# Batch 1's queries and keys re-cut: a shorter first part transposed together with the end of batch 0, and a last block of 96 tokens in step 23

## The chip, the core and the metric

One core of a Trainium2 chip (trn2) runs the whole program. The metric is device time in microseconds (us) of one execution; the median of three runs is the figure given. PE is the matmul engine (TensorE), DVE the vector engine, ACT the scalar engine, POOL the GpSimd engine, SP the engine that only issues transfers. PSUM is the memory that PE writes and that ACT and DVE copy out of.

## The reference

Attention over a window of 32 tokens to either side for 8 batches, 8 heads, 576 tokens and head size 64, then a two-layer block with an ELU on the 4608 x 512 result:

```
scores = q @ k.T / sqrt(64), outside |i - j| <= 32 set to -1e9
attn   = exp(scores - max) / (sum + 1e-9)
x      = (attn @ v), heads side by side: 4608 x 512
h      = x @ w_in                      # 512 x 2048
g      = where(h > 0, h, exp(min(h, 0)) - 1)
out    = g @ w_out                     # 2048 x 512
```

## The kernel before

The tokens are cut into 36 pairs of 2 x 64 queries; a batch of 576 tokens is 4.5 pairs, so pair 4 holds the last 64 queries of batch 0 and the first 64 of batch 1, and pair 5 holds queries 64 to 191 of batch 1. One pair is `scores` (L371, 16 small matmuls), `exponential` (L392, ACT), `mask` (L399, DVE), `pv` (L408, 16 small matmuls), `normalize` (L422, DVE), and then a transpose of the result on PE with a copy out of PSUM (`x_transpose` L433 and `x_evac` L450) or, from pair 10 on, by a transfer.

The two-layer block runs in 144 steps (loop at L840). Step kk does `elu` of the step before on DVE, then `mm1(kk)` (eight matmuls of 256 columns, L734), `exponents` (ACT, L744), `subtract` (L756), and then `mm2` of an earlier step (four matmuls of 512 columns, L787). The work of the pairs, the casts, the transposes and the later loads are put by hand between these: `at(kk, slot, fn, ...)` (L568) files a task, and the loop runs it. The slots of one step stand in this order: "first", `elu`, "dve", the first half of mm1, "half", the second half of mm1 and its `exponents` and `subtract`, "mid", then the mm2's (a slot that is a number stands ahead of the mm2 of that number: in step 8 slot 6 lies between mm2(5) and mm2(6)), "end". Each engine keeps this order; nothing is reordered later.

q and k come in token-major and are needed head-size-major. Tokens are placed so that partition c of 32 holds nj tokens that follow each other, and one 128-column transpose is made for each j of nj. There are two ways in. `load_cast` (L137) lets POOL issue a transfer that casts to bf16; each j then takes two transposes of 64 columns (L335). `load_qk` (L123) lets SP load fp32, `cast_qk` (L294) casts on ACT or DVE, and each j takes one full transpose (L340). `transpose_qk` (L327) makes the transposes into one PSUM tile and copies that tile into `qT` or `kT` with one copy (`evict`, L344, on the engine that it is given; with `later` the copies come after all the transposes).

Batch 1 is cut into two halves of 288 tokens: `HALF_A = (0, 9)` by `load_cast` (L548), transposed in step 8 (q, slot 6) and step 9 (k, slot "half"), both copied out by ACT; `HALF_B` by `load_qk` (L559), cast in steps 14 and 15, transposed at the end of steps 15 and 16. The last 64 queries and 32 keys of batch 0 (`FRONT_C`) are transposed by `transpose_late` (L592) in step 6. Pair 4's `scores` and `exponential` stand at the end of step 9, pair 5's in step 12, pairs 6 and 7 from step 18, pairs 8 and 9 from step 26 (L621 to L641).

PSUM tiles go by tag, and each tag has one buffer: "s" and "u" hold 1024 fp32 for each of 128 partitions and serve the pairs' scores and results and the transposes; "h0" and "h1" serve mm1 of even and odd steps. A tile of a tag is written only when the copy or the read of that tag's last tile is done. From pair 6 on, even pairs use "s" and odd pairs "u", and `x_transpose` writes into its pair's tag: pair 7's is filed at the end of step 22, in "u". In steps 22 to 25 batch 2's q and k are transposed in four groups of nine, with the tags "s", "u", "s", "u" (steps 22 mid, 23 end, 24 mid, 25 mid), all copied out by ACT.

POOL issues its transfers in the order of the code: batch 1's two casting loads lie between parts of w_in and w_out and ahead of batch 1's v. SP waits at a small transfer (`gate`, L191) for the last part of w_in, and then issues HALF_B of batch 1 and the whole of batch 2.

Of the kernel before, what the change touches and what calls it, by code (L numbers as in the profile page):

```python
# [10 lines left out]
BF16 = mybir.dt.bfloat16  # L11
# [4 lines left out]
def _bap(ap, new_ap, off=0):  # L16
    return bass.AP(tensor=ap.tensor, offset=ap.offset + off,
                   ap=[list(x) for x in new_ap])
# [3 lines left out]
def kernel(  # L22
# [9 lines left out]
    nc = tc.nc  # L32

    B, H, S, D = q.shape
# [9 lines left out]
    HP = H // 2  # L44
    NC = 128 // HP
# [15 lines left out]
    cpool = ctx.enter_context(tc.tile_pool(name="const", bufs=1))  # L61
# [32 lines left out]
    def ps_tile(shape, dt, tag, name):  # L94
        return pools[tag].tile(shape, dt, tag=tag, name=name)
# [21 lines left out]
    HJ = SJ // 2  # L117
    WHOLE, HALF_A, HALF_B = (0, SJ), (0, HJ), (NC * HJ, HJ)
    FRONT_B = ((NC * HJ, HJ - 2), (NC * HJ, HJ - 1))
    FRONT_C = ((NC * (SJ - 2), 2), (NC * (SJ - 1), 1))  # L120
    qk_f = {}

    def load_qk(b, which, part, engs=(nc.sync, nc.sync)):  # L123
        z, nj = part
        mj = max(nj, HJ)
        t = lpool.tile([128, 2, mj * D], FP32, tag=f"f{which}{mj}",
                       name=f"f{which}", bufs=2 if part is WHOLE else 1)
        qk_f[b, which, z] = t
        src = (q, k)[which][b, :, z:z + NC * nj, :].rearrange(
            "(g h) (c j) d -> c g h (j d)", h=2, j=nj)  # L130
        for h in range(2):
            engs[h].dma_start(out=t[:, h, 0:nj * D], in_=src[:, :, h, :])
# [4 lines left out]
    def load_cast(b, which, part):  # L137
        z, nj = part
        mj = nj if nj < 3 else HJ + 1
        t = cpool.tile([128, 2, mj * D], BF16, tag=f"c{which}{mj}",  # L140
                       name=f"c{which}")[:, :, 0:nj * D]
        qk_c[b, which, z] = t
        src = (q, k)[which][b, :, z:z + NC * nj, :].rearrange(
            "(g h) (c j) d -> c g h (j d)", h=2, j=nj)
        nc.gpsimd.dma_start(out=t, in_=src)

    def load_v(b, m, rows=(0, 128)):
        lo = 128 * m - WIN
        p0 = max(rows[0], -lo)
        p1 = min(rows[1], S - lo)  # L150
        nc.gpsimd.dma_start(  # L151
            out=V_e[b % 3][p0:p1, m, :, 0:D],
            in_=v[b, :, lo + p0:lo + p1, :].rearrange("h p d -> p h d"))
# [37 lines left out]
    def gate(src, dt=BF16, eng=nc.sync):  # L191
        gates[0] += 1
        t = cpool.tile([1, 1], dt, name=f"gate{gates[0]}")
        eng.dma_start(out=t, in_=src)

    def load_w_in(c, z=0, nz=1):
        w = D_FF // 4 // nz
        c = c * nz + z
        nc.gpsimd.dma_start(
            out=w_in_sb[:, :, c * w:(c + 1) * w],  # L200
            in_=moe_w_in[:, c * w:(c + 1) * w].rearrange(
                "(o p) f -> p o f", p=128))

    def load_w_out(c, z=0, nz=1):
        n = NFO // 4 // nz
        c = c * nz + z
        nc.gpsimd.dma_start(
            out=w_out_sb[:, c * n:(c + 1) * n, :],
            in_=moe_w_out[c * n * 128:(c + 1) * n * 128, :].rearrange(
                "(o p) f -> p o f", p=128))  # L210

    def w_in_at(c):
        return w_in_sb[0:1, 0, (c + 1) * (D_FF // 4) - 1:(c + 1) * (D_FF // 4)]
# [7 lines left out]
    def edges(i):  # L221
# [8 lines left out]
    ident = cpool.tile([128, 128], BF16)  # L230
# [15 lines left out]
        out=far, in_=far, compare_op=ALU.is_ge, fill=FAR,  # L246
        base=0, pattern=[[0, 2], [-1, QB]], channel_multiplier=1)
    nc.gpsimd.affine_select(
        out=far, in_=far, compare_op=ALU.is_ge, fill=FAR,
        base=2 * WIN, pattern=[[0, 2], [1, QB]], channel_multiplier=-1)  # L250
    nc.gpsimd.affine_select(
        out=far[:, 0, :], in_=far[:, 0, :], compare_op=ALU.is_ge, fill=FAR,
# [35 lines left out]
    def copy_on(eng, d_, s_):  # L288
        if eng is nc.scalar:
            nc.scalar.copy(d_, s_)  # L290
        else:
            eng.tensor_copy(d_, s_)  # L292
# [15 lines left out]
    def keys_or_queries(b, which):  # L308
        if which == 0:
            return qT[b % 2].rearrange("p g s -> p (g s)")  # L310
        return kT[b % 2][:, KPAD:KPAD + HP * S]
# [15 lines left out]
    def transpose_qk(b, which, part, j0, n, evac, tag="t0", later=None,  # L327
                     pt=None):
        z, nj = part
        if pt is None:  # L330
            pt = ps_tile([128, 1024 if n <= 8 else 2048], BF16, tag, "ptx")
        for j in range(n):
            if (b, which, z) in qk_c:
                for h in range(2):
                    nc.tensor.transpose(  # L335
                        pt[64 * h:64 * (h + 1), j * 128:(j + 1) * 128],
                        qk_c[b, which, z][:, h, (j0 + j) * D:
                                          (j0 + j + 1) * D], ident)
            else:
                nc.tensor.transpose(  # L340
                    pt[:, j * 128:(j + 1) * 128],
                    qk_b[b, which, z][:, j0 + j, :], ident)

        def evict(d=None, rows=NC, pitch=S):  # L344
            d = keys_or_queries(b, which) if d is None else d
            copy_on(evac,
                    _bap(d, [d.ap[0], [pitch, HP], [nj, rows], [1, n]],
                         z + j0),
                    _bap(pt, [pt.ap[0], [1, HP], [HP, rows], [128, n]]))

        if later is None:
            evict()
        else:
            later.append(evict)
# [132 lines left out]
    for which in range(2):  # L487
        load_cast(0, which, FRONT_B[which])
# [9 lines left out]
    for which in range(2):  # L498
        load_cast(0, which, FRONT_C[which])
    load_w_out(1)  # L500
# [3 lines left out]
    BOTH = (nc.scalar, nc.vector)  # L504
# [40 lines left out]

    load_w_in(2, 0, 2)
    for which in range(2):
        load_cast(1, which, HALF_A)  # L548
    load_w_in(2, 1, 2)
    load_w_out(2)  # L550
    for m in range(3):
# [2 lines left out]
    load_w_out(3)  # L554
    for m in range(3, VS):
        load_v(1, m)
    gate(w_in_at(3))
    for which in range(2):
        load_qk(1, which, HALF_B)  # L559
    for which in range(2):  # L560
        load_qk(2, which, WHOLE)

# [5 lines left out]
    def at(kk, slot, fn, *args):  # L568
        tasks.setdefault((kk, slot), []).append((fn, args))
# [19 lines left out]
    at(1, "mid", x_transpose, 3, "y1")  # L589
    at(1, "mid", x_evac, 3, nc.vector)  # L590
    at(5, "dve", swap_pools)
    def transpose_late(tag):  # L592
        pt = ps_tile([128, 2, 512], BF16, tag, "ptx")
        evicts = []
        for which in range(2):
            transpose_qk(0, which, FRONT_C[which], 0, FRONT_C[which][1],
                         BOTH[which], later=evicts, pt=pt[:, which, :])
        for evict in evicts:
            evict()

    at(6, "mid", transpose_late, "s")
    at(6, "dve", rotate_back, 0, 3, 4, (1,))

    for which in range(2):
        at(8 + which, (6, "half")[which], transpose_qk, 1, which, HALF_A, 0,
           HJ, nc.scalar, "s")
        at(14 + which, "mid", cast_qk, 1, which, HALF_B, 0, HJ, BOTH[which])
        at(15 + which, "end", transpose_qk, 1, which, HALF_B, 0, HJ,
           nc.scalar, "s")
    at(6, "dve", edges, 2)  # L610
    at(16, "dve", hold_v, 2)
# [12 lines left out]
    for i in range(4, NPAIR):  # L624
        two = i >= FIRST_TWO
        kk, z = begin[i], i % 2 if two else 0
        at(kk, "end" if i == 4 else "mid", scores, i,
           "u" if z else "s")
        at(kk + z, "end" if i == 4 else "mid", exponential, i)
        at(kk + 1 + z, "dve", mask, i)  # L630
        at(kk + (2 if two else 1), "end", pv, i)
        n = kk + (3 + z if two else 2)
        at(n, "dve", normalize, i)
        if i < FIRST_DMA:

            x_at = (n + 1, "half") if i == 5 else (n, "end")
            at(*x_at, x_transpose, i)
            at(*x_at, x_evac, i, nc.scalar)
        else:
            at(n, "end", x_dma, i)  # L640
# [248 lines left out]
```

## Time and profile before

| what | value |
|---|---|
| median of three runs | 302.49 us (302.11 to 302.96) |
| the profiled execution's own time | 302.52 us |
| its span, first to last instruction | 300.8 us |
| PE busy | 291.8 us, 97% of the span |
| DVE busy | 240.9 us, 80% |
| ACT busy | 170.2 us, 57% |
| granted clock of PE | 0.999 |
| casting loads of batch 1 (q and k) | 288 KB each, 8.2 and 8.3 us from issue to landing |
| loads of HALF_B (q, k) | issued at 39.70 and 41.03 us, 4.8 to 5.1 us to landing |

A line of the timeline holds the start (us from the span's start), the duration, the engine, the line of the code, the operation, what is written from what, the shapes and the count. "[0.42 <-PE ps L734]" says that the engine stood idle for 0.42 us before it and what ended that. A matmul's duration runs to its end in the pipeline, so it is longer than its slot: the distance from one start to the next says what PE spends. Some matmul records are missing, so a group of four can read "x3" and start late.

### The profile page before, as it was taken

How to read it: one execution, taken by the hardware profiler on the slowest of the kernel's cores; microseconds unless marked ns; L12 is line 12 of the kernel's file. 1: busy time of each engine (PE TensorE's matmuls, PEld its weight loads, DVE VectorE, ACT ScalarE, POOL GpSimd, SP SyncE). 2: the span in 40 equal slices, each digit the busy share in tenths (PEclk: the TensorE clock that was granted, in tenths of full speed). 3: DMA queues.
4: the chain of work that ended last, by engine and by line, in shares of the span. 5: the costliest groups of instructions: out<-in, count | busy, mean ns of one | idle time of the engine just before them, and what ended most of it. 6: DMA issues, size and time to landing. Idle time of an engine off the chain costs nothing.

```text
span 300.8 us, 7664 instructions
## 1 busy us (share of the span) xinstructions
PE 291.8 (97%) x3066; PEld 198.6 (66%) x3118; DVE 240.9 (80%) x479; ACT 170.2 (57%) x258; POOL 52.7 (18%) x74
## 2 busy tenths in 40 slices
PE   7899999999999999999999999999999999999995
PEld 3585567677666666666666666666666666666673
DVE  7788588978787988888889789887988787877773
ACT  3783648688655567456745665467535353534342
POOL 8777203520005000410032002300000000000000
PEclk9999999999999999999999999999999999999999
DMA  9999999999957978999899989997921111111011
GB/s 190 168 200 203 185 233 349 370 179 231 241 159 199 239 116 270 244 267 135 161 256 323 172 203 252 312 153 137 268 54 72 35 72 38 70 37 70 2 70 71
DMA packets 94070, 52.68 MB, mean 175 GB/s; under 512 B 78163, under 2 KB 83795, under 8 KB 94035
## 3 DMA queue, kind: packets, MB, share of 16 engines
q1 hardware_dynamic: 47330, 35.61, 44.7%
q0 software_dynamic: 44976, 10.10, 44.2%
q10 hardware_dynamic: 1728, 6.49, 6.3%
q8 instruction: 24, 0.39, 0.6%
q14 instruction: 12, 0.09, 0.1%
HBM read 36.70 MB, written 15.34 MB: 173 GB/s over the span
## 4 chain that ended last, share of the span: by engine, by line
PE 85%; DMA 5%; issue 3%; DVE 2%; ACT 2%; POOL 2%; POOLq 0%; ACTq 0%; DVEq 0%
PE ps L734 39%; PE psY L787 38%; PE psS L416 4%; DMA out_dram<-y_sb 3%; PE psS L384 3%; DMA c<-in_k_dram 2%; ACT e_sb L744 1%; DVE g_sb L767 1%; PE ptx L335 1%; PE psXT L438 1%; POOL Vo L158 1%; DVE qkb L292 0%; ACT qkb L290 0%; PE ptx L340 0%; PE psS L364 0%
## 5 line engine op out<-in xcount | busy, mean ns | idle before, releaser
L744 ACT ACTIVATE e_sb<-ps 128x512 f32<-128x512 f32 (+1 forms) x145 | 86.3, 596 | 113.4 <-PE ps L734 106.0
L734 PE MATMUL ps<-xT,w_in_sb 128*128 128x256 bf16 (+1 forms) x1168 | 149.7, 271 | 0.1
L787 PE MATMUL psY<-w_out_sb,g_sb 128*128 128x512 bf16 (+2 forms) x541 | 139.3, 373 | 2.9 <-issue 0.3
L734 PEld LDWEIGHTS <-w_in_sb 128*128 128x128 bf16 x1168 | 110.4, 98 | 36.8 <-issue 0.8
L767 DVE SCALAR_TENSOR_TENSOR g_sb<-ps,m_sb 128x512 bf16<-128x512 f32 (+1 forms) x145 | 99.3, 686 | 13.1 <-DVE m_sb L756 0.5
L756 DVE TENSOR_SCALAR m_sb<-e_sb 128x512 bf16<-128x512 f32 (+1 forms) x142 | 61.5, 433 | 34.3 <-ACT e_sb L744 32.3
L787 PEld LDWEIGHTS <-g_sb 128*128 128x128 bf16 x592 | 55.9, 98 | 38.7
L151 POOL DMA_DIRECT2D Ve<-in_v_dram x37 | 32.5, 892 | 132.8 <-PE psS L416 79.5
L395 ACT ACTIVATE pu<-psS 128x1024 bf16<-128x1024 f32 x36 | 36.6, 1023 | 0.9 <-PE psS L384 0.8
L428 DVE TENSOR_TENSOR x_st<-psS,rc 128x512 bf16<-128x512 f32 x36 | 24.9, 692 | 1.2
L290 ACT CAST qkb<-f 128x768 bf16<-128x768 f32 (+1 forms) x29 | 25.0, 862 | 0.0
L404 DVE TENSOR_TENSOR pm<-pu,masks 128x1024 bf16<-128x1024 bf16 x32 | 21.8, 682 | 0.0
L416 PEld LDWEIGHTS <-pm 128*64 128x64 bf16 x512 | 9.6, 110 | 7.3 <-DVE pm L404 6.5
L292 DVE COPY y_sb<-psY 128x512 f32<-128x512 f32 (+1 forms) x18 | 12.2, 676 | 1.5 <-PE psY L787 1.5
L384 PEld LDWEIGHTS <-kT 64*128 64x128 bf16 x560 | 9.4, 95 | 4.6 <-issue 4.4
L290 ACT COPY y_sb<-psY 128x512 f32<-128x512 f32 (+1 forms) x19 | 10.8, 569 | 2.5 <-PE psY L787 2.5
L384 PE MATMUL psS<-qT,kT 64*128 64x64 bf16 x560 | 11.8, 191 | 0.1
L416 PE MATMUL psS<-Ve,pm 128*64 128x65 bf16 x288 | 11.5, 196 | 0.1
L290 ACT COPY qT<-ptx 128x1152 bf16<-128x1152 bf16 (+4 forms) x9 | 7.7, 882 | 5.0 <-PE ptx L340 3.5
L416 PE MATMUL psS<-Vo,pm 128*64 128x65 bf16 x224 | 10.3, 196 | 0.0
L175 DVE COPY Vo<-Ve 64x1040 bf16<-64x1040 bf16 (+1 forms) x22 | 9.1, 413 | 0.7
L425 DVE RECIPROCAL rc<-psS 128x8 f32<-128x8 f32 x36 | 7.2, 199 | 0.9 <-PE psS L416 0.9
(54 smaller groups left out, 91.3 us busy)
## 6 DMA issues: line engine op xcount, KB each, us to landing
out_dram<-y_sb SPq DMA_DIRECT2D x36, 256.0 KB, 3.5
f<-in_q_dram SPq DMA_DIRECT2D x12, 576.0 KB, 6.3
f<-in_k_dram SPq DMA_DIRECT2D x12, 576.0 KB, 8.0
in_dram<-qkb ACTq DMA_DIRECT2D x10, 576.0 KB, 4.2
Ve<-in_v_dram POOLq DMA_DIRECT2D x21, 128.0 KB, 12.6
w_out_sb<-in_moe_w_out_dram POOLq DMA_DIRECT2D x3, 512.0 KB, 10.4
Ve<-in_v_dram POOLq DMA_DIRECT2D x14, 96.0 KB, 11.6
w_in_sb<-in_moe_w_in_dram POOLq DMA_DIRECT2D x2, 512.0 KB, 10.4
```

Source lines behind the costliest of these rows:

```text
L151: nc.gpsimd.dma_start(out=V_e[b % 3][p0:p1, m, :, 0:D], in_=v[b, :, lo + p0:lo + p1, :].rearrange("h p d -> p h d"))
L290: nc.scalar.copy(d_, s_)
L384: nc.tensor.matmul(psS[:, h % 2, hp * 128 + z * QB:hp * 128 + (z + 1) * QB], lhsT=keys, rhs=qT[b % 2][base:base + 64, hp, QB * qb:QB * (qb ...
L395: nc.scalar.activation(pu, _bap(psS, [psS.ap[0], [1, 1024]]), AX.Exp, scale=SCALE)
L404: nc.vector.tensor_mul(pm, pu, _bap(mm, [mm.ap[0], [0, H], [1, 2 * QB]]))
L416: nc.tensor.matmul(psS[QB * z:QB * (z + 1), par, hp * VD:(hp + 1) * VD], lhsT=pm[:, par * HP + hp, z * QB:(z + 1) * QB], rhs=vv[:, qb // 2 ...
L428: nc.vector.tensor_mul(x_st, _bap(psS, [psS.ap[0], [VD, HP], [512, 2], [1, D]]), _bap(rc, [rc.ap[0], [2, HP], [1, 2], [0, D]]))
L734: nc.tensor.matmul(o, lhsT=w_in_sb[:, do, fo * 128:(fo + 1) * 128], rhs=r, start=(do == 0), stop=(do == NDO - 1))
L744: nc.scalar.activation(e_sb, ps, AX.Exp)
L756: nc.vector.tensor_scalar(m_sb, e_sb, -1.0, None, ALU.add)
L767: nc.vector.scalar_tensor_tensor(g_t[kk][:, z * w:(z + 1) * w, :], ps, 0.0, m_t.pop((kk, z)), ALU.max, ALU.min)
L787: nc.tensor.matmul(sum_of(t, ts, c), lhsT=g_t[n][:, j, ts * 128:(ts + 1) * 128], rhs=w_out_sb[:, s * FG + j, cols_of(c)], start=(s == 0 an ...
```

## The change

Batch 1 is cut in three. `ONE_A`, by `load_cast`, holds only what pairs 4 and 5 read: 192 queries (nj = 6) and 224 keys (nj = 7). `ONE_B`, by `load_qk`, are the next 288 queries and keys (nj = 9, as before). The last 96 tokens come in as a block of their own, `load_last`: 96 tokens on 96 partitions, all heads side by side, cast to bf16 by two transfers that POOL issues behind batch 1's v; `transpose_last` makes four transposes of it (96 columns each) and one copy; of the keys only the last 64 tokens are copied.

`transpose_late` of step 6 and the two tasks of steps 8 and 9 become one, `transpose_casts`, in step 8, slot 6: 26 transposes of ONE_A and the 6 of FRONT_C into one tile of tag "s", and after all of them four copies (batch 1: queries on DVE, keys on ACT; batch 0: queries on ACT, keys on DVE). Pair 4's `scores` and `exponential` move from the end of step 9 to its "mid", ahead of mm2(7). `transpose_last` stands in step 23: queries at "half" in tag "u", copied by ACT, keys at "mid" in tag "s", copied by DVE.

```diff
+    ONE_A = (0, 6), (0, 7)
+    ONE_B = tuple((NC * nj, HJ) for _, nj in ONE_A)
+    LAST = 3 * NC
...
+    def load_last(b, which):
+        last[which] = cpool.tile([LAST, H * D], BF16, name=f"last{which}")
+        nc.gpsimd.dma_start(
+            out=last[which].rearrange("p (h d) -> p h d", h=H),
+            in_=(q, k)[which][b, :, S - LAST:S, :].rearrange("h p d -> p h d"))
+
+    def transpose_last(b, which, z, evac, tag):
+        pt = ps_tile([128, HP, LAST], BF16, tag, "ptx")
+        for g in range(HP):
+            nc.tensor.transpose(pt[:, g, :],
+                                last[which][:, 2 * g * D:2 * (g + 1) * D],
+                                ident[0:LAST, 0:LAST])
+        copy_on(evac, keys_or_queries(b, which).rearrange(
+            "x (g s) -> x g s", g=HP)[:, :, z:S], pt[:, :, z - S + LAST:LAST])
...
-        load_cast(1, which, HALF_A)
+        load_cast(1, which, ONE_A[which])
...
+    for which in range(2):
+        load_last(1, which)
     gate(w_in_at(3))
     for which in range(2):
-        load_qk(1, which, HALF_B)
+        load_qk(1, which, ONE_B[which])
...
-    def transpose_late(tag):
-        pt = ps_tile([128, 2, 512], BF16, tag, "ptx")
-        evicts = []
-        for which in range(2):
-            transpose_qk(0, which, FRONT_C[which], 0, FRONT_C[which][1],
-                         BOTH[which], later=evicts, pt=pt[:, which, :])
+    def transpose_casts(tag):
+        pt = ps_tile([128, 2048], BF16, tag, "ptx")
+        n, evicts = 0, []
+        for b, parts, evacs in ((1, ONE_A, (nc.vector, nc.scalar)),
+                                (0, FRONT_C, BOTH)):
+            for which in range(2):
+                nj = parts[which][1]
+                transpose_qk(b, which, parts[which], 0, nj, evacs[which],
+                             later=evicts, pt=pt[:, n * 128:(n + nj) * 128])
+                n += nj
         for evict in evicts:
             evict()
-    at(6, "mid", transpose_late, "s")
+    at(8, 6, transpose_casts, "s")
+    for which in range(2):
+        at(23, ("half", "mid")[which], transpose_last, 1, which,
+           NC * (ONE_A[which][1] + HJ), BOTH[which], "us"[which])
...
-        at(8 + which, (6, "half")[which], transpose_qk, 1, which, HALF_A, 0,
-           HJ, nc.scalar, "s")
...
-        at(kk, "end" if i == 4 else "mid", scores, i,
-           "u" if z else "s")
-        at(kk + z, "end" if i == 4 else "mid", exponential, i)
+        at(kk, "mid", scores, i, "u" if z else "s")
+        at(kk + z, "mid", exponential, i)
```

More of the change, by code (lines that the diff above doesn't have):

```diff
@@ L145, in load_cast @@
         nc.gpsimd.dma_start(out=t, in_=src)
+    last = {}
+    def load_last(b, which):
[11 more added lines that the diff above has]
+            "x (g s) -> x g s", g=HP)[:, :, z:S], pt[:, :, z - S + LAST:LAST])
     def load_v(b, m, rows=(0, 128)):
@@ L591 @@
     at(5, "dve", swap_pools)
-    def transpose_late(tag):
-        pt = ps_tile([128, 2, 512], BF16, tag, "ptx")
-        evicts = []
-        for which in range(2):
-            transpose_qk(0, which, FRONT_C[which], 0, FRONT_C[which][1],
-                         BOTH[which], later=evicts, pt=pt[:, which, :])
+    def transpose_casts(tag):
[8 more added lines that the diff above has]
+                n += nj
         for evict in evicts:
             evict()
-    at(6, "mid", transpose_late, "s")
+    at(8, 6, transpose_casts, "s")
+    for which in range(2):
+        at(23, ("half", "mid")[which], transpose_last, 1, which,
+           NC * (ONE_A[which][1] + HJ), BOTH[which], "us"[which])
     at(6, "dve", rotate_back, 0, 3, 4, (1,))
     for which in range(2):
-        at(8 + which, (6, "half")[which], transpose_qk, 1, which, HALF_A, 0,
-           HJ, nc.scalar, "s")
-        at(14 + which, "mid", cast_qk, 1, which, HALF_B, 0, HJ, BOTH[which])
-        at(15 + which, "end", transpose_qk, 1, which, HALF_B, 0, HJ,
+        at(14 + which, "mid", cast_qk, 1, which, ONE_B[which], 0, HJ,
+           BOTH[which])
+        at(15 + which, "end", transpose_qk, 1, which, ONE_B[which], 0, HJ,
            nc.scalar, "s")
```

## The prediction, made before the changed kernel ran

> **What bounds the kernel now.** I read the page first: shares by engine, then the chain that ended last.
>
> ```profile
> PE 291.8 (97%) x3066; PEld 198.6 (66%) x3118; DVE 240.9 (80%) x479; ACT 170.2 (57%) x258; POOL 52.7 (18%) x74
> ...
> PE 85%; DMA 5%; issue 3%; DVE 2%; ACT 2%; POOL 2%; POOLq 0%; ACTq 0%; DVEq 0%
> ```
>
> PE is the bound. From step 26 on it is so without a break: the chain in order of time has mm1 groups that follow a long pause of pair work at 109.36, 124.68, 140.00 and 155.32 us, 15.32 us apart each time. So a microsecond that PE loses before 70 us should come out at the end, and one saved too. The change lies between 24 and 66 us; I read the timeline there, start to start.
>
> ```profile
> 27.45 0.43 DVE L756 TENSOR_SCALAR m_sb<-e_sb 128x512 bf16<-128x512 f32 x1
> ...
> 27.79 0.28 DVE L292 COPY kT<-ptx 128x128 bf16<-128x128 bf16 x1
> 27.99 0.68 DVE L767 SCALAR_TENSOR_TENSOR g_sb<-ps,m_sb 128x512 bf16<-128x512 f32 x1
> ...
> 28.82 1.03 PE L734 MATMUL ps<-xT,w_in_sb 128*128 128x256 bf16 x8
> ...
> 30.64 0.69 PE L335 MATMUL ptx<-ident,c 128*64 128x128 bf16 x18
> 31.27 1.04 PE L787 MATMUL psY<-w_out_sb,g_sb 128*128 128x512 bf16 x4
> 31.38 1.12 ACT L290 COPY qT<-ptx 128x1152 bf16<-128x1152 bf16 x1 [0.89 <-PE ptx L335]
> ...
> 32.67 0.69 PE L335 MATMUL ptx<-ident,c 128*64 128x128 bf16 x18
> ...
> 34.71 0.41 PE L384 MATMUL psS<-qT,kT 64*128 64x64 bf16 x16
> ...
> 35.05 1.05 PE L734 MATMUL ps<-xT,w_in_sb 128*128 128x256 bf16 x8
> ...
> 37.03 0.34 PEld L416 LDWEIGHTS <-pm 128*64 128x64 bf16 x16 [0.56 <-DVE pm L404]
> ```
>
> See the slots: mm1 or mm2 of a step is 0.87 us, 18 half-width transposes 0.63 (35 ns each), 16 scores 0.34; a switch to a narrow form costs about 0.1. mm1(8) starts at 28.82 although mm2(4), begun at 27.74, needs only 0.87: PE stands 0.21 us for elu(6), the DVE line at 27.99. mm1(10) is at 35.05, and pair 4's pv at 37.03 waits some 0.14 us for its mask.
>
> The other place is step 23.
>
> ```profile
> 62.93 1.29 ACT L290 COPY qT<-ptx 128x1152 bf16<-128x1152 bf16 x1
> 62.94 0.39 PE L438 MATMUL psXT<-ident,x_st 128*128 128x128 bf16 x4
> ...
> 63.17 1.04 PE L734 MATMUL ps<-xT,w_in_sb 128*128 128x256 bf16 x8
> ...
> 64.04 1.03 PE L787 MATMUL psY<-w_out_sb,g_sb 128*128 128x512 bf16 x4
> 64.08 0.60 ACT L290 COPY xT<-psXT 128x512 bf16<-128x512 bf16 x1
> 64.55 0.63 ACT L744 ACTIVATE e_sb<-ps 128x512 f32<-128x512 f32 x1
> ```
>
> mm1(23) runs from 63.17 to 64.04. Pair 7's transposed result went into tag "u" at 62.94, but ACT copies it out only at 64.08, behind the 1.29 us copy of batch 2's queries, until 64.68. Nobody waits for that now: the next writer of "u" comes at 64.90.
>
> [...] The trace of before shows no two copies of one tile side by side; the changed program as built orders them (below). [...] here both kinds were in flight from 39.70 to 44.0 us.
>
> **Loads (POOL, SP).** ONE_A's two transfers carry 192 + 224 KB for 576. The casting loads landed at 28.55 (20.35 + 8.2) and 29.9 (21.61 + 8.3), some 1.4 us apart for 288 KB, so what POOL queues behind lands about 0.8 us earlier (160/288 x 1.4, estimate). No gain: the transposes at 30.64 were not late for data, and w_in's last part (gate at 38.81) was in time for mm1(12) at 39.38. load_last adds two issues on POOL, 0.8 us each, behind v; POOL then stands until 49.66. They move 768 small pieces each, like the last v load, which landed 0.7 us after the one ahead of it (44.0 against 43.3). So they land by about 45 us and are read at 63. SP's queue has the same transfers; batch 2's queries land at 49.2 (42.25 + 6.9) for a cast at 54.23, so 0.8 us of contention is hidden. If that cover were gone, the cost would be what exceeds 5 us. ONE_B has HALF_B's sizes: steps 14 to 16 cost the same.
>
> **Step 6.** Six transposes go: 0.29 us on PE, about 0.4 with the switch, a copy each on ACT (0.37) and DVE (0.28). No gain: mm1(8) waits for elu(6), and elu(6) starts 0.54 after its subtract (27.45), the usual distance of the two (36.89 to 37.41, 41.29 to 41.82), so the 0.28 copy lay in a gap. mm1(8) stays at 28.82. From below the saving is zero, from above 0.2 us.
>
> **Steps 8 to 10.** 32 transposes from 30.64 last 32 x 35 ns = 1.12: mm2(6) at 31.76, mm1(9) at 32.63 (no "half" now: 0.73 saved), PE ready for pair 4's scores at 33.50 + 0.1 = 33.60. But the scores need all four copies, and in the built order these are one chain: each waits by semaphore for the one before where the engine changes, and the first for all 32 transposes. Start 31.87 (0.11 behind, as 31.27 to 31.38). DVE, 768 columns: 0.97 by the line through 282 and 698 ns. ACT, 896: 0.91 (368 and 1120); ACT, 256: 0.35 back to back; DVE, 128: 0.28; two changes of engine and the way to PE at 0.04 to 0.05 each. 31.87 + 2.51 + 0.12 = 34.50: PE stands 0.90 us. On DVE elu(8) is queued behind this chain (34.45 to 35.14), on ACT exponents(9); mm1(10) needs elu(8), and comes later. Then scores 0.34, mm2(7) 0.87: mm1(10) at 35.71, 0.66 later than now. Scores ahead of mm2(7) bring the mask early (exp from 34.94, mask done about 37.1), so pv's 0.14 goes: pv at 37.55 against 37.03. **+0.52 us.** The first copy is not in the trace: if it ran as fast as DVE's contiguous 512-column copy (425 ns in the groups by form), 0.55, this would be +0.1; with all copies 5% slower, +0.65. I take the strided rate, since its input steps by 128.
>
> **Step 23.** "half" comes at 63.17 + 0.44 = 63.61. The transposes write "u", and the built order has the first of them wait for ACT's copy of pair 7: 64.68 + 0.06 = 64.74. PE stands **1.13 us**; queued behind it are half of mm1(23) and mm2(21). Four transposes at 40 to 55 ns each: 0.2, and again 0.2 for the keys (their "s" is free at 64.22). **+1.53 us.** ACT's order up to that copy is unchanged and is paced by PE (it waits for pair 6's transposes at 60.90), so step 8's shift moves both. Behind: ACT's new copy (384 columns, 0.48) is over at 65.5, before "u" is next written at 66.4; DVE's (256 columns, 0.28 to 0.42) comes behind subtract(23). ACT waited 0.42 us for PE at 65.61 and can fall in step again, so I put nothing more.
>
> **Sum**, against the profiled execution's 302.52 (span 300.8 and 1.72 around it; the median 302.49 is 0.03 less): 302.52 + 0.52 + 1.53 = 304.57, **304.6 us**, 0.7% more. About 0.3% can be told from no change; that is 303.4.
>
> **Rivals.**
> (a) Copies of step 8 overlap: ACT's pair beside DVE's is over at about 33.2, before 33.60. Then the scores wait for nothing and pv comes at 36.65, -0.38: 302.52 - 0.38 + 1.53 = 303.7. For it: in the trace different tiles are copied side by side (7.69 and 7.92 us). Against: the built waits.
> (b) No wait at step 23: 302.52 + 0.52 + 0.4 = 303.4. For it: only ACT's lag makes it. Against: the copy at 64.08 stands behind work that the change leaves alone.
> (c) Knock-on: ACT and DVE are near full from 61 to 72 us; elu(25) ended at 71.93 for mm1(27) at 72.35, 0.42 us of room. Twice 0.5 more: 305.6.
> (d) Not slower: later waits take it up. If PE, after step 26, waited for something with a time of its own (a load, a transposing transfer) for 2 us in all, the shift would vanish there: 302.5. It decides "same" from 1.2 us on. Against: the even 15.32 us.
> That the change is not what it says is excluded by the built order.
>
> **Chances.** Forecast 0.64 (304.0 to 305.2), a 0.10, b 0.07, c 0.11, d 0.08. Slower: forecast, a (nearly all), half of b, and c: 0.87; same 0.12; faster 0.01. The range 303.4 to 305.7 leaves out d, half of b and tails.
>
> **What would show it.** PE idle of 0.9 us ahead of L406 of pair 4 with DVE's copy of kT ending just before; mm1(8) unmoved; pv's wait gone; in step 23 about 1.1 us between the halves of mm1(23), ended by ACT's copy to xT; the shift constant from step 26. Wrong if copies overlap, if mm1(8) comes earlier, or if the shift changes after 75 us.

## The result and the profile after

The changed kernel takes 304.41 us (median of six runs, 304.01 to 305.37) where the kernel before takes 302.22 on the same chip: ratio 1.0074, 95% interval 1.0055 to 1.0094, so it is slower by about 2.2 us. The profiled execution took 304.54 us with a span of 302.8, against 302.52 and 300.8. The predicted 304.6 is met; the parts that it was summed from are met only in part.

From the page of the changed kernel: busy time of each engine, the chain that ended last, and one group by lines.

```profile
PE 290.6 (96%) x3064; PEld 198.1 (65%) x3116; DVE 241.6 (80%) x481; ACT 169.1 (56%) x258; POOL 53.6 (18%) x76
...
PE 80%; DMA 11%; POOL 3%; issue 2%; ACT 2%; DVE 0%; SPq 0%; POOLq 0%; ACTq 0%
...
L312 ACT CAST qkb<-f 128x768 bf16<-128x768 f32 (+1 forms) x29 | 25.0, 861 | 1.6 <-DMA f<-in_q_dram 1.6
```

PE is busy for 1.2 us less in a span that is 2.0 us longer. The chain has 11% of transfers where it had 5%, and the wait in the last line is new: ACT once stood 1.6 us before a cast, waiting for a load of queries (0.0 in that group before). The prediction has no such wait. The timeline of the changed kernel around step 8 comes first (start, duration, engine, line, what; in brackets the idle time ahead and what ended it):

```profile
27.63 1.03 PE L764 MATMUL ps<-xT,w_in_sb 128*128 128x256 bf16 x8
...
29.46 1.08 PE L357 MATMUL ptx<-ident,c 128*64 128x128 bf16 x32
...
30.58 0.96 DVE L314 COPY qT<-ptx 128x768 bf16<-128x768 bf16 x1 [0.82 <-PE ptx L357]
...
31.58 0.91 ACT L312 COPY kT<-ptx 128x896 bf16<-128x896 bf16 x1 [2.28 <-DVE qT L314]
32.38 0.38 ACT L312 COPY qT<-ptx 128x256 bf16<-128x256 bf16 x1
...
32.79 0.29 DVE L314 COPY kT<-ptx 128x128 bf16<-128x128 bf16 x1 [1.25 <-ACT qT L312]
...
33.14 0.41 PE L406 MATMUL psS<-qT,kT 64*128 64x64 bf16 x16 [0.75 <-DVE kT L314]
...
36.18 0.45 PE L438 MATMUL psS<-Ve,pm 128*64 128x65 bf16 x16
```

The four copies stand one behind the other: ACT's first names DVE's copy as its releaser, DVE's second names ACT's, and PE's scores (L406) name that one, after 0.75 us of idle. This is the chain that was forecast. Then the place that was not, in a later stretch of the same timeline:

```profile
33.09 0.78 POOL L156 DMA_DIRECT2D last<-in_q_dram  x1 [1.83 <-DMA w_out_sb<-in_moe_w_out_dram]
...
33.87 0.77 POOL L156 DMA_DIRECT2D last<-in_k_dram  x1
...
38.89 1.22 SPq L137 DMA_DIRECT2D f<-in_q_dram  x2
...
46.20 1.15 ACT L312 CAST qkb<-f 128x1152 bf16<-128x1152 f32 x1 [1.59 <-DMA f<-in_q_dram]
...
47.89 0.66 PE L362 MATMUL ptx<-ident,qkb 128*128 128x128 bf16 x9 [1.09 <-ACT xT L312]
```

ONE_B's queries are issued from 38.89 us and are not there when ACT wants to cast them at 44.6; ACT stands 1.59 us, a copy queued behind the cast is late, and PE stands 1.09 us for it. The two transfers of the last block had been issued five to six us earlier. The view of the transfers (KB each, us from issue to landing) of the changed kernel gives their times:

```profile
f<-in_q_dram SPq DMA_DIRECT2D x2, 288.0 KB, 6.3
...
last<-in_q_dram POOLq DMA_DIRECT2D x1, 96.0 KB, 10.6
last<-in_k_dram POOLq DMA_DIRECT2D x1, 96.0 KB, 10.5
```

and the same view of the kernel before has, for loads of the same size, line and order:

```profile
f<-in_q_dram SPq DMA_DIRECT2D x2, 288.0 KB, 4.8
```

So the last block is in flight until 43.7 and 44.4 us, beside ONE_B's loads, and these take 1.5 us longer. In the kernel before, ACT casts HALF_B's queries without a wait for their load:

```profile
45.36 1.15 ACT L290 CAST qkb<-f 128x1152 bf16<-128x1152 f32 x1
```

Step 23 in the changed kernel:

```profile
63.56 1.28 ACT L312 COPY qT<-ptx 128x1152 bf16<-128x1152 bf16 x1
...
63.79 0.60 PE L764 MATMUL ps<-xT,w_in_sb 128*128 128x256 bf16 x4
...
64.70 0.60 ACT L312 COPY xT<-psXT 128x512 bf16<-128x512 bf16 x1
65.35 0.33 PE L163 MATMUL ptx<-ident,last 96*128 96x96 bf16 x4 [0.96 <-ACT xT L312]
...
65.52 0.60 PE L764 MATMUL ps<-xT,w_in_sb 128*128 128x256 bf16 x4
...
65.96 0.34 PE L163 MATMUL ptx<-ident,last 96*128 96x96 bf16 x4
66.13 1.03 PE L817 MATMUL psY<-w_out_sb,g_sb 128*128 128x512 bf16 x3
```

The first half of mm1(23) is done at 63.79 + 0.44 = 64.23; the transposes into "u" wait for ACT's copy of pair 7 (64.70, done 65.30) and start at 65.35, 1.12 us later. Each group of four then takes 0.17.

The distances between starts on PE, read from the timelines of all kernels of this case, put the whole span in one table (us; "pv(4)" is pair 4's group at L438 of the changed kernel, L416 of the one before; the first column is the start of mm1(6); the kernels e1 to e10 are described in the next section):

| kernel | mm1(6) | to pv(4) | to mm1(16) | to mm1(22) | to mm1(24) | to mm1(26) | to the end |
|---|---|---|---|---|---|---|---|
| before | 23.87 | 13.16 | 10.96 | 12.71 | 4.71 | 4.51 | 230.88 |
| after | 23.05 | 13.13 | 12.21 | 12.94 | 6.17 | 4.47 | 230.83 |
| e1_late_last | 23.66 | 13.39 | 11.96 | 12.94 | 6.16 | 4.48 | 230.9 |
| e4_before_loads | 24.13 | 12.95 | 13.13 | 14.25 | 4.70 | 4.48 | 230.86 |
| e8_before_held_loads | 23.06 | 13.03 | 11.05 | 12.81 | 4.71 | 4.47 | 230.87 |
| e5_held_last | 24.26 | 13.08 | 10.96 | 12.79 | 6.16 | 4.58 | 230.97 |
| e3_early_batch0 | 23.32 | 12.31 | 12.91 | 12.94 | 6.16 | 4.48 | 230.88 |
| e6_held_early | 23.93 | 12.30 | 10.96 | 12.79 | 6.16 | 4.48 | 230.88 |
| e2_lasts_mid_s | 23.42 | 13.14 | 11.29 | 12.93 | 5.27 | 4.48 | 230.87 |
| e7_held_early_mid | 23.22 | 12.30 | 11.26 | 12.78 | 6.31 | 4.48 | 230.95 |
| e9_held13 | 23.18 | 12.29 | 11.24 | 12.71 | 5.27 | 4.51 | 231.3 |
| e10_no_last | 23.28 | 12.48 | 11.70 | 13.03 | 4.70 | 4.48 | 230.83 |

After minus before: -0.82 - 0.03 + 1.25 + 0.23 + 1.46 - 0.04 - 0.05 = +2.00, the difference of the spans. The first column is not the change's: before's cut of the loads gives anything from 23.06 to 24.13 there, the new cut 23.05 to 24.26. Nor is the +1.25 the same in every execution: e2_lasts_mid_s, which is the changed kernel up to step 23, has 11.29 in the column "to mm1(16)", +0.33, and e1_late_last +1.00. The row of e4_before_loads is that of an execution of 306.23 us, well above that kernel's median of 303.41, so its sizes are not compared with the other rows.

### The profile page after: what moved, and what is told of

It reads as the page before. It is cut to its first block, busy times and chain, and to the rows that moved or that the text cites. A ratio compares the mean times of both kernels' runs of the same rounds, so it can differ in the third digit from the quotient of the medians.

```text
span 302.8 us, 7663 instructions
## 1 busy us (share of the span) xinstructions
PE 290.6 (96%) x3064; PEld 198.1 (65%) x3116; DVE 241.6 (80%) x481; ACT 169.1 (56%) x258; POOL 53.6 (18%) x76
## 3 DMA queue, kind: packets, MB, share of 16 engines
q0 software_dynamic: 46544, 10.13, 46.1%
## 4 chain that ended last, share of the span: by engine, by line
PE 80%; DMA 11%; POOL 3%; issue 2%; ACT 2%; DVE 0%; SPq 0%; POOLq 0%; ACTq 0%
PE ps L764 36%; PE psY L817 36%; DMA w_in_sb<-in_moe_w_in_dram 6%; PE psS L438 3%; PE psS L406 3%; DMA Vo<-in_v_dram 2%; DMA f<-in_q_dram 2%; POOL Vo L180 1%; PE ptx L362 1%; POOL c L150 1%; ACT qkb L312 0%; ACT qT L312 0%; ACT e_sb L774 0%; ACT xT L312 0%; PE psXT L460 0%
## 5 line engine op out<-in xcount | busy, mean ns | idle before, releaser
L438 PEld LDWEIGHTS <-pm 128*64 128x64 bf16 x512 | 9.7, 110 | 7.2 <-DVE pm L426 5.9
L406 PEld LDWEIGHTS <-kT 64*128 64x128 bf16 x560 | 9.4, 95 | 5.7 <-issue 3.9
L406 PE MATMUL psS<-qT,kT 64*128 64x64 bf16 x560 | 11.9, 191 | 1.3 <-DVE kT L314 1.0
L438 PE MATMUL psS<-Ve,pm 128*64 128x65 bf16 x288 | 11.5, 196 | 0.0
L438 PE MATMUL psS<-Vo,pm 128*64 128x65 bf16 x224 | 10.3, 196 | 0.0
```

Source lines behind the costliest of these rows:

```text
L406: nc.tensor.matmul(psS[:, h % 2, hp * 128 + z * QB:hp * 128 + (z + 1) * QB], lhsT=keys, rhs=qT[b % 2][base:base + 64, hp, QB * qb:QB * (qb ...
L438: nc.tensor.matmul(psS[QB * z:QB * (z + 1), par, hp * VD:(hp + 1) * VD], lhsT=pm[:, par * HP + hp, z * QB:(z + 1) * QB], rhs=vv[:, qb // 2 ...
```

## The experiments

Theory before the first runs: three things cost time, the chain of copies of step 8, the late landing of ONE_B because of the last block's transfers, and the wait for "u" in step 23. Rival for the second: ONE_B is late only because PE came 0.8 us early in that one execution. The median of before on the same chip stands in brackets.

### The last block's transfers

**e1_late_last**: the changed kernel, with the last block's loads filed in step 15.

```diff
-    for which in range(2):
-        load_last(1, which)
     gate(w_in_at(3))
...
+    for which in range(2):
+        at(15, "end", load_last, 1, which)
```

> The changed kernel with one difference: the two transfers of the last 96 tokens are issued by POOL at the end of step 15, when ONE_B has landed, and no longer behind batch 1's v. Contention theory (they share the DMA engines with ONE_B's loads, which then took 6.1 to 6.8 us instead of 4.8 to 5.1): ONE_B's queries land about 5 us after issue, ACT's wait of 1.6 us for them in step 14 is gone or below 0.5, and the time is about 1 us below the changed kernel's: 303.2 to 303.6 us. Rival (PE only came early because the opening stretch happened to be 1.2 us shorter in the execution profiled, and ONE_B would be waited for anyway): no gain, 304.2 to 304.6.

Measured: 304.69 [302.25], ratio 1.0092 (1.0059 to 1.0125). The edit did nothing. The profile of this kernel, POOL and ACT in the timeline:

```profile
33.19 0.77 POOL L156 DMA_DIRECT2D last<-in_q_dram  x1 [1.20 <-DMA w_out_sb<-in_moe_w_out_dram]
...
46.82 1.15 ACT L312 CAST qkb<-f 128x1152 bf16<-128x1152 f32 x1 [1.34 <-DMA f<-in_q_dram]
```

A task filed late in the program is not late on an engine that has nothing to wait for: POOL ran ahead and issued at 33.19. So this is a second execution of the change, and useful as one: its mm1(6) is only 0.21 earlier than before's, and ONE_B's queries still landed 6.5 to 6.7 us after their issue. That speaks against the rival of the early PE; e4 and e8 settle it.

**e4_before_loads**: the kernel before, with the last block's two transfers added behind v, into tiles that nobody reads.

```diff
+    for which in range(2):
+        t = cpool.tile([96, H * D], BF16, name=f"last{which}")
+        nc.gpsimd.dma_start(
+            out=t.rearrange("p (h d) -> p h d", h=H),
+            in_=(q, k)[which][1, :, S - 96:S, :].rearrange("h p d -> p h d"))
     gate(w_in_at(3))
```

> The kernel before with one addition: the two transfers of batch 1's last 96 tokens, issued by POOL behind batch 1's v, into tiles that nothing reads. Contention theory: HALF_B's loads take 6 us and more instead of 4.8 to 5.1, its cast in step 14, which had some 0.3 us of room, comes about 1 us late, and PE loses 0.5 to 1 us: 302.7 to 303.3. Rival (hidden, as predicted): 302.2 and no wait at that cast.

Measured: 303.41 [302.25], ratio 1.0065 (1.0035 to 1.0095); the profiled execution took 306.23. From ACT's waits in it, between 20 and 76 us (us in all, times, longest):

```profile
ACT qkb L290 <- DMA f<-in_q_dram: 2.5, 1, 2.5
```

HALF_B's queries landed 7.1 to 7.2 us after their issue, against 4.8 without the added transfers. By the medians two transfers of 96 KB, 768 pieces each, cost the kernel before some 1.2 us by themselves, and this with mm1(6) at 24.13, later than in the kernel before.

The profiled execution lost more. PE stood 2.01 us for the late copy behind that cast, and then ran at a lower granted clock (PEclk) for a while; the view of this stretch:

```profile
core 0: us, PE busy (x) PEld busy (x) DVE busy (x) ACT busy (x) POOL busy (x), PEclk, DMA share, GB/s
51.00:54.00 3.00, 3.00 (x16) 1.71 (x15) 1.93 (x5) 1.72 (x3) 1.68 (x2) 0.50 1.01 408
```

From mm1(16) to mm1(17) PE took 3.91 us where it took 2.24 before: this, and no load, is the +1.54 of e4's column up to mm1(22). In e3 below PE stood 1.77 us at the same place and the clock stayed at 1.00; what decides it is not shown.

**e5_held_last**: the changed kernel, with a write by DVE into the tiles in step 15, so that the transfers can't be issued earlier.

```diff
+    def hold_last():
+        for which in range(2):
+            last[which] = cpool.tile([LAST, H * D], BF16, name=f"last{which}")
+            nc.vector.memset(last[which][0:1, 0:1], 0.0)
...
+    at(15, "dve", hold_last)
+    for which in range(2):
+        at(15, "end", load_last, 1, which)
```

> The changed kernel, with the two transfers of the last 96 tokens really held back: DVE clears one element of each tile in step 15, and POOL's transfers wait for that. (In e1 nothing held them: POOL issued them at 33.19 and 34.53 us, as in the changed kernel, so e1 told nothing.) Contention theory: ONE_B's queries land about 5 us after issue instead of 6.1 to 6.8, ACT's wait for them in step 14 falls from 1.6 to below 0.6 us, and the time is 303.3 to 303.7 us. Rival (ONE_B is late on its own, since PE comes early): no gain, 304.2 to 304.6.

Measured: 303.88 [302.04], ratio 1.0057 (1.0042 to 1.0071). The timeline of this kernel shows that the hold works:

```profile
47.56 0.78 POOL L160 DMA_DIRECT2D last<-in_q_dram  x1 [15.30 <-DVE last L157]
```

ONE_B's queries landed in 4.4 us (the keys in 6.3, but nothing waits for them), ACT waits for no load, and the stretch from pv(4) to mm1(16) is 10.96, as before. Against the change this is 1.0074 - 1.0057 = 0.17%, 0.5 us, and not the 1.25 us of the one profiled execution of the change; the intervals overlap, so the size is less sure than the stage.

**e8_before_held_loads**: the kernel before with the same two unread transfers, held like this.

```diff
+    at(15, "dve", hold_last)
+    for which in range(2):
+        at(15, "end", load_last, 1, which)
```

> The kernel before with the two transfers of the last 96 tokens into tiles that nothing reads, held back by DVE until step 15. In e4 the same transfers issued behind batch 1's v cost 1.2 us and HALF_B's queries took 7.1 us to land. Theory (it is only their time, beside HALF_B's loads, that costs): HALF_B's queries land in about 4.8 us again, and the time is that of the kernel before, 302.1 to 302.5. Rival (the added transfers cost wherever they lie, through batch 2's loads or POOL's queue): 302.8 to 303.4.

Measured: 302.36 [302.04], ratio 1.0014 (1.0004 to 1.0023); HALF_B's queries landed in 4.6 to 4.7 us. The same bytes at another time cost 0.3 us and not 1.2: what e4 pays for is where they lie, beside HALF_B. And PE was as early here as in the change (mm1(6) at 23.06), yet ACT waited only 0.2 us for the load and mm1(16) came 0.09 us later than before, counted from pv(4). So an early PE alone is not the cause.

### The chain of copies

**e3_early_batch0**: the end of batch 0 goes back to step 6, and batch 1's two copies of step 8 are both made by ACT.

```diff
-    at(8, 6, transpose_casts, "s")
+    at(6, "mid", transpose_casts, "s", 0, FRONT_C, BOTH)
+    at(8, 6, transpose_casts, "s", 1, ONE_A, (nc.scalar, nc.scalar))
```

> The changed kernel with one difference: the end of batch 0 is transposed in step 6 again, in its own tile, and step 8 transposes batch 1's part alone, both copies on ACT, so that no copy waits for one on another engine. Theory (chain of four copies holds pair 4's scores for 0.9 to 1 us): about 1.65 us of copies after 26 transposes, done before PE wants the scores; that wait is gone, and the 6 transposes of step 6 cost nothing, since PE waits there for elu(6) anyway. Pair 4's pv comes 0.8 to 1.0 us earlier, counted from mm1(8). In the end 303.4 to 303.7 us if PE doesn't lose it again, but if ONE_B's late landing in step 14 holds PE then, part or all of it is lost there: up to 304.4. Rival (the wait was for data or for PE's own order): no change before pv.

Measured: 304.31 [302.25], ratio 1.0063 (1.0047 to 1.0079), no different from the change. The timeline of this kernel:

```profile
30.85 0.80 ACT L312 COPY qT<-ptx 128x768 bf16<-128x768 bf16 x1 [1.12 <-PE ptx L357]
31.55 0.91 ACT L312 COPY kT<-ptx 128x896 bf16<-128x896 bf16 x1
32.58 0.41 PE L406 MATMUL psS<-qT,kT 64*128 64x64 bf16 x16
...
46.35 1.15 ACT L312 CAST qkb<-f 128x1152 bf16<-128x1152 f32 x1 [2.28 <-DMA f<-in_q_dram]
```

The scores wait for nothing now, and pv(4) comes 0.82 us sooner after mm1(6) than in the change. 0.70 of it is lost again up to mm1(16): at the cast ACT stands 2.28 us where it stood 1.59. While the load is this late, what the chain costs doesn't show at the end.

**e6_held_early**: e5_held_last and e3_early_batch0 together.

```diff
+    at(15, "dve", hold_last)
...
+    at(6, "mid", transpose_casts, "s", 0, FRONT_C, BOTH)
+    at(8, 6, transpose_casts, "s", 1, ONE_A, (nc.scalar, nc.scalar))
```

> e5, and besides the end of batch 0 in step 6 again with batch 1's copies both on ACT, as in e3. In e3 the 0.8 us that PE gained before pair 4's pv was lost at ONE_B's cast in step 14, where the wait grew from 1.6 to 2.3 us. Theory (the wait for ONE_B hid what the chain of copies costs): with ONE_B on time the chain's cost shows, and this is 0.4 to 0.9 us below e5: 302.5 to 303.2. Rival (the chain costs nothing anyway): the time of e5.

Measured: 303.20 [302.04], ratio 1.0036 (1.0022 to 1.0050), 0.68 us under e5, with intervals that touch. With ONE_B on time, the 0.78 us that the table shows up to pv(4) stay. Against e3, which differs only in the hold, it is 0.27% or 0.8 us less. Up to pv(4) this order is also 0.86 us shorter than the kernel before (12.30 against 13.16): the shorter first part does save time, which the change lost again.

### Step 23

**e2_lasts_mid_s**: the changed kernel, with both last blocks at the "mid" of step 23, in one tile of tag "s", both copied by DVE.

```diff
-    for which in range(2):
-        at(23, ("half", "mid")[which], transpose_last, 1, which,
-           NC * (ONE_A[which][1] + HJ), BOTH[which], "us"[which])
+    at(23, "mid", transpose_lasts, "s")
```

> The changed kernel with one difference: both blocks of the last 96 tokens are transposed at the mid of step 23 into one tile of tag s, both copied by DVE, so that nothing at the half of step 23 waits for ACT's copy of pair 7 out of tag u. Theory (PE stands 1.13 us at that half): about 0.2 us of waiting is left (tag s is released about 0.2 us after PE gets there), so 0.9 to 1.0 us less than the changed kernel: 303.4 to 303.6 us. Rival (PE waits there because ACT and DVE are behind in steps 21 to 25 altogether, and the wait turns up one or two steps later): the same, 304.2 to 304.5.

Measured: 303.17 [302.25], ratio 1.0036 (1.0021 to 1.0051), 1.24 us under the change. PE in the timeline of this kernel:

```profile
63.25 1.04 PE L775 MATMUL ps<-xT,w_in_sb 128*128 128x256 bf16 x8
64.34 0.50 PE L635 MATMUL ptx<-ident,last 96*128 96x96 bf16 x8
64.68 1.03 PE L828 MATMUL psY<-w_out_sb,g_sb 128*128 128x512 bf16 x4
```

mm1(23) is whole again. Eight transposes take 0.34 us, 0.22 are lost ahead of them, and the step is 0.56 longer than before instead of 1.46. The work is cheap; 0.9 us of it was waiting for ACT's copy out of "u". Tag, place in the step and copying engine changed together here; that the wait was for that copy is read from the change's own trace.

The rest of the 1.24 us lies ahead of step 23, where this kernel is the change itself. ONE_B was issued at 38.59 in this execution, 0.30 us sooner than in the change's, while PE reached mm1(15) 0.38 us later, and ACT waited less:

```profile
45.66 1.15 ACT L312 CAST qkb<-f 128x1152 bf16<-128x1152 f32 x1 [0.67 <-DMA f<-in_q_dram]
```

**e7_held_early_mid**: e6_held_early and e2_lasts_mid_s together.

```diff
+    at(15, "dve", hold_last)
...
+    at(6, "mid", transpose_casts, "s", 0, FRONT_C, BOTH)
+    at(8, 6, transpose_casts, "s", 1, ONE_A, (nc.scalar, nc.scalar))
+    at(23, "mid", transpose_lasts, "s")
```

> e6, and besides both last blocks at the mid of step 23 in tag s, both copied by DVE, as in e2. In e2 that was worth 1.2 us. If the three costs are separate and add up, 301.3 to 302.0 us, at or a little below the kernel before. If the wait at step 23 only took up what ACT and DVE lack anyway, no less than e6: 302.5 to 303.2.

Measured: 302.80 [302.04], ratio 1.0019 (1.0007 to 1.0032): a miss, the sum of the three was not reached. PE's weight loads in step 23 of this kernel wait:

```profile
PEld L636 <- DMA last<-in_k_dram: 1.0, 1, 1.0
```

Held until step 15, the last block is queued with batch 2's loads and takes up to 17.5 us, until 64.3. The wait for the tag is now a wait for data.

**e9_held13**: e7_held_early_mid, released two steps sooner.

```diff
-    at(15, "dve", hold_last)
+    at(13, "dve", hold_last)
...
-        at(15, "end", load_last, 1, which)
+        at(13, "end", load_last, 1, which)
```

> e7 with one difference: the transfers of the last 96 tokens are released in step 13 (about 42 us) and no longer in step 15. In e7 PE stood 0.9 us in step 23 for their data, which landed at 60 and 64 us (14 to 17 us after issue, among batch 2's loads). Theory (only that is left): they land by about 60 us, that wait is gone, ONE_B's queries still land some 5 us after issue, and the time is 301.4 to 302.0 us against 302.0 for the kernel before. If releasing them 3 us earlier puts them beside ONE_B's loads again, PE waits in step 14 and the time is that of e7 or more, 302.6 to 303.2.

Measured: 302.68 [302.26], ratio 1.0016 (0.9991 to 1.0041): no difference from the kernel before can be told, and the 301.4 to 302.0 of the theory were missed. Step 23 costs 0.56. The last block was issued while ONE_B was in flight, but behind it and not ahead of it:

```profile
41.34 0.77 POOL L160 DMA_DIRECT2D last<-in_q_dram  x1 [9.05 <-DVE last L157]
```

ONE_B's queries, issued from 38.95, landed in 4.4 us all the same. But the waits of PE's weight loads from 34 to 44 us have, as in e7, a new line:

```profile
PEld L779 <- DMA w_in_sb<-in_moe_w_in_dram: 0.3, 1, 0.3
```

PE is now early enough for mm1(12) to wait for w_in's last part, and 0.28 us is lost up to mm1(16).

**e10_no_last**: no last block. ONE_B holds all the rest of batch 1 (12 and 11 tokens per partition, 384 and 352 KB), with the steps 6 and 8 of e3.

```diff
-    ONE_B = tuple((NC * nj, HJ) for _, nj in ONE_A)
+    ONE_B = tuple((NC * nj, SJ - nj) for _, nj in ONE_A)
...
-    for which in range(2):
-        load_last(1, which)
```

> e3 without any block of its own for the last tokens: ONE_B takes them too (nj = 12 for the queries, 11 for the keys, fp32 loads of 384 and 352 KB for 288), so that no small pieces are loaded and nothing is added in step 23; step 6 and step 8 as in e3. Theory: the early saving of 0.75 us up to pair 4's pv stays, the five full transposes more cost 0.28 us, ONE_B's larger loads some 0.3 us of waiting in step 14, step 23 costs what it did before: 301.5 to 302.2 us. Rival (ONE_B's landing sets step 14 whatever the pieces are, and larger loads land later still): PE loses 1 us and more in step 14, 302.5 to 303.5.

Measured: 302.57 [302.26], ratio 1.0005 (0.9989 to 1.0020), the same as before: the rival's range, not the theory's. PE saves 0.68 us up to pv(4) and gives 0.74 back up to mm1(16); ACT waits 0.6 us for ONE_B. Step 23 is untouched.

## Why the prediction came out as it did

- **Step 6**, "zero, from above 0.2 us": measured at the upper end. From mm1(6) to mm1(8) the kernels with transposes in step 6 take 4.73 to 4.95 us (eight executions, median 4.74), those without 4.53, 4.58, 4.59 and 4.84. So some 0.16 us, read from one execution of each, with groups that overlap. The reason given holds: from elu(5) to elu(6) DVE takes 3.47 us in both profiles, with the copy and without it. What was left out is that PE doesn't always wait for elu(6): in five of the eight mm1(8) starts 1.73 to 1.75 us after mm1(7), which is mm1 and mm2 without a pause, and there the transposes on PE do cost. The sign "mm1(8) comes earlier" thus came true in part.
- **Steps 8 to 10**, +0.52: right in mechanism, 0.18 too large. From mm1(8) to pv(4) it is 8.21 before and 8.55 after, +0.34. From the first transpose to the scores I had 3.86 us; it took 33.14 - 29.46 = 3.68. The copies had the durations that I gave them (0.96, 0.91, 0.38 and 0.29 for 0.97, 0.91, 0.35 and 0.28), which were worked out from the trace of before: DVE 282 ns for 128 columns and 698 for 512 strided ones, ACT 368 for 256 and 1120 for 1152. The changes of engine took 0.04 and 0.03 us and the way to PE 0.06. But the first began 0.11 us sooner than put, and ACT's second began 0.80 us after its first, not 0.91 + a gap. The rival of overlapping copies (a) is refuted by the brackets. In the change's trace no two copies of the tile run side by side on different engines: DVE's first ends at 31.54 us and ACT's first starts at 31.58, ACT's second ends at 32.76 and DVE's second starts at 32.79. No run leaves that order out, so what copies of one tile on two engines would do without it was not shown.
- **Loads**: this is the step that failed. "ONE_B has HALF_B's sizes: steps 14 to 16 cost the same", and the contention of 0.8 us was called hidden because batch 2's queries have 5 us of room. I gave the room of the wrong load. ONE_B stands between, and it had 0.3 us: HALF_B's queries landed at 40.3 + 4.8 = 45.1 us and were cast at 45.36. In place of zero three profiles of these transfers show +1.25 (the change), +1.00 (e1) and +0.33 us (e2) up to mm1(16), and 0.22 or 0.23 behind it, in steps 16 to 22; held back, the two transfers make the whole 0.5 us shorter in e5 and 0.8 in e6. That is near an estimate from the parts: 1.5 us longer to landing, less 0.3 of room, less the 0.8 us that POOL's queue comes sooner, as predicted (the gate at 37.45 to 38.61 with the new cut, 38.50 to 39.23 with the old), is 0.4. e4 and e8 show the cause by themselves: the same transfers cost 1.2 us beside HALF_B and 0.3 when they are issued 12.5 us later (33.89 and 46.40).
- **Step 23**, +1.53: measured +1.46, with 1.12 us of wait for 1.13. Rival (b) is refuted; e2 shows that the wait and not the work is what costs.
- **Behind it**: from mm1(26) on all kernels but e9 (231.3) take 230.8 to 231.0 us, so nothing is added or taken up there. Rivals (c) and (d) fail for what is lost in step 23. But (d)'s mechanism acts earlier, where I had not put it: before step 16, w_in's last part and ONE_B pace PE, and time saved ahead of them is taken back (e3 nearly wholly, 0.70 of 0.82 us against the change; e10 wholly, 0.74 for 0.68 against before, with a larger ONE_B besides; e9 in part, 0.28 of 0.87 against before).

**The sum** was right for a mixed reason. I had +2.05; the two profiles give +2.00, of which step 23 is +1.46, the load +1.48 with its sequel, steps 6 to 10 -0.03, the rest -0.09, and -0.82 a front that happened to run early. A term that I left out and one that chance put in nearly cancel. In the medians, +2.2, no single early front counts, and the load, which an early PE waits for the longer (e3, with pv(4) at 35.63 us, has 2.28 us of ACT's wait, the change, with pv(4) at 36.18, 1.59), is worth less: step 23's 1.46, 0.5 for the load (e5) and 0.18 from steps 6 to 10 (0.34 less 0.16) make 2.1, an estimate. There too a load put at nothing and steps 6 to 10 put 0.34 too high cancel. The total was met in part by luck.

How the two kinds of loads share the DMA engines shows in the packets. In the 3 us from ONE_B's first issue (38.89 us) the change has 2798 packets on q0 and 39 (0.09 MB) on q1; in the 3 us from HALF_B's (39.70) the kernel before has 1661 and 158 (0.33 MB). q0 is the queue that the last block adds to (44976 packets in the whole span before, 46544 after); q1 alone has packets from 44.0 to 46.2 us (339 in the change), where the view lists SP's loads only. That fits a load that is slowed as long as q0 is full: in the change the last block is in flight until 44.4 us and the load lands some 1.7 us later, at 46.1. No run here shows how an engine chooses between the queues, and whether the number of pieces (768 each) or the bytes matter stays open: the pieces were not made larger. Two tiles of different tags for step 8's copies were not tried either.

## What to carry to other kernels

For each transfer that is added, list every load in flight in the same window with the room at its reader, and price the one with the least room, not the largest (here ONE_B with 0.3 us, not batch 2 with 5). Filing an issue in a later step of the program need not delay it: in e1 it did not (33.19 us, 33.09 in the change), in e5 a write that it had to wait for did (47.56). A small block put in the middle of a PE-bound step can cost far more than its work (here 1.12 us of wait for 0.34 of transposes): ask who empties its PSUM tag, and what stands ahead of that copy. And time saved ahead of a load that is only just in time may not be saved, as in e3 (0.82 us saved, 0.70 lost again).

## What the runs showed of the hardware that was not expected

- Two transfers of 96 KB in 768 small pieces each raised the landing of 288 KB loads of queries issued some five us later from 4.8 us to between 6.1 and 7.2 us. Issued 2.4 us behind the first of these loads (e9) they did not: 4.4 us. Issued among batch 2's loads, the small ones themselves took 13.6 to 17.7 us (e5 to e8).
- In one execution (e4) the granted clock of PE fell to 0.50 for some 3 us after PE had stood for 2.01 us; after 1.77 us (e3) it did not.
- The records of ACT's copies that follow each other without a wait overlap: the second started 0.80 us after a first of 0.91 (and 0.70 after one of 0.80 in e3).
- The start of mm1(6) varies by 1.2 us (23.05 to 24.26) between executions of programs whose work on PE is alike up to there, while from mm1(26) to the end the spread is 0.2 us in all but one.
